# TensorE used as two engines of 64 rows, from the first projection to the end of attention

## The chip, the cores and the metric

The kernel runs on one core of a Trainium2 chip. The metric is the device time of one execution in microseconds (us). Three runs of the kernel before took 1952.63, 1952.87 and 1954.74 us; the median is 1952.87 us.

A core has a matrix engine (TensorE, PE in the profile) that multiplies a stationary operand, loaded by a weight load (PEld), with a moving operand that streams past it; three engines for elementwise work (VectorE or DVE, ScalarE or ACT, GpSimd or POOL); and queues that issue DMA transfers (SP's, here, carries nearly all). Operands lie in SBUF, with the contraction on its 128 partitions; products are accumulated in PSUM and moved out by ACT or DVE.

## The reference

x is 2048 tokens by 576 features. The block computes attention and a gated MLP on the same normalised input.

```python
xn = layernorm(x)
# A: sliding-window attention, 32 heads of 18, window 256, causal
q, k, v = split_heads(xn @ wqkv)                 # wqkv: 576 x 1728
scores = einsum("bhqd,bhkd->bhqk", q, k) * 18**-0.5
p = softmax(where(0 <= i - j < 256, scores, -1e9))
s = merge_heads(p @ v) @ wo
# B: gMLP
z = gelu(xn @ w_in)                              # w_in: 576 x 4608
z1, z2 = z[..., :2304], layernorm(z[..., 2304:])
g = w_sp @ z2 + b_sp                             # over tokens, 2048 x 2048
return x + s * silu((z1 * g) @ w_out)
```

## The kernel before, in words

Every projection is computed from a high and a low part: a value is rounded (`split`, L112: ACT copies with rounding, DVE subtracts) and the product is hi*hi + hi*lo + lo*hi. The normalised input is kept transposed, features on partitions, as nine "planes" in the six tiles b0 to b5 (`plane`, L185): four high planes of 128 features, four low ones, and one that holds the last 64 features, high part above and low part below. A projection of 576 features is then the 14 matmuls that `passes` yields: three for each of four planes, and two for the ninth plane, whose two halves hold different parts.

The stages, in order:

1. Queries and keys (`qk_chunk`, L293): for each of four chunks of 512 tokens the input is normalised and transposed (`norm_chunk`), then nine blocks of 128 columns of q and k are formed by 14 matmuls of 512 tokens each (L312; the first two blocks at L306). Each result is split and stored to DRAM (st_d) in an order that puts a head's 18 features side by side. Weights come in by `load_wqkv`.
2. Values (`v_matmuls`, L504): 16 token tiles, 14 x 2 matmuls of 288 columns each, stored to v_d. They fill gaps of stage 1; what is left follows it.
3. z2 (L720): six pieces of 384 columns by 16 token tiles, 14 matmuls each, then gelu and the statistics of the second layernorm. POOL meanwhile forms sums of blocks of w_sp (`sp_combos`). Near the end the row maxima of the first attention unit are taken.
4. Attention and z1 together (the loop from L796): 16 units, each four heads by half of the tokens. A unit has 32 row-maximum products (`row_max`, L428: queries stationary, keys moving, 128 x 384 or 128 x 256; DVE adds the mask and takes the maximum, L432), a negated maximum that goes out through DRAM and back into two more rows of the query tile, score products (`scores`, L554: keys stationary, queries moving, up to 384 columns; ACT takes the exponential, L558; POOL cuts the band's edges, L562 and L565) and the products with the values (`pv`, L578), in which four heads of 32 output columns each stand side by side in the array. A head's q and k hold 56 rows of 128 (hi and lo parts, the maximum and ones); the other rows of its query tile are zero, so that a 128-row matmul takes one head. z1 = 18 blocks of 128 columns by four chunks of 512 tokens by 14 matmuls (L484) fills the time between.
5. The output projection (L910), the spatial product over tokens (L1150) and the final projection (L1243).

In stages 3 and 4 the order on PE, POOL and DVE is the order in which the program issues the work (`manual_schedule`); in stage 4 ACT and SP too. In stage 4 a small planner writes that order: it keeps a clock, adds an assumed cost for each matmul (`spend`; MM = 227 ns for 512 columns), keeps assumed times at which ACT and DVE will be done, gives every score and maximum product a due time spread over the unit, and fills with z1 matmuls whenever none is due or ready. Score products and row-maximum products have two PSUM banks each (`tps`, `sps`), z1 has two (`mmp`). Products with the values are made for two key blocks at a time (PVN).

## Time and profile before

| | |
|---|---|
| median of three runs | 1952.87 us (1952.63 to 1954.74) |
| span of the profiled execution | 1949.2 us |
| its instructions | 30859, of them 11159 matmuls and as many weight loads |
| PE busy / DVE / ACT / POOL | 1931.0 / 1050.1 / 897.2 / 283.5 us |

The profile gives the profiled execution by its span, from its first to its last instruction; the median of the runs is 3.7 us longer than that, and what lies around the span of this one execution is not shown apart. In the profile "mean ns of one" of a matmul is its latency, from its start to a modelled end; matmuls overlap, so that the time that one costs in a row of them is read from the distance of starts, or from a merged piece of the chain of work. A row like "L720 PE MATMUL mm<-z2wh,b 128*128 128x384 x720" reads: line 720, stationary operand of 128 rows by 128 columns, 384 moving columns, 720 times.

### The profile page before, as it was taken

The numbers are of one execution on the slowest core, as the hardware profiler recorded it, in microseconds if no ns is written. First come the engines' busy times: TensorE is split into PE (matmuls) and PEld (weight loads), VectorE is DVE, ScalarE is ACT, GpSimd is POOL, SyncE is SP. The second block draws the span as 40 slices with busy tenths as digits, with TensorE's granted clock in tenths as the row PEclk, the third lists the DMA queues.
The fourth block names the chain that finished last, engine by engine and source line by source line (L and its number), as shares of the span: only waits on it lengthen the run. The fifth ranks groups of instructions, "written<-read, shape, count | busy, mean of one in ns | idle before, by whom it ended". The sixth has DMA issues, their size and how long they took to land.

```text
span 1949.2 us, 30859 instructions
## 1 busy us (share of the span) xinstructions
PE 1931.0 (99%) x11159; PEld 1656.4 (85%) x11159; DVE 1050.1 (54%) x2294; ACT 897.2 (46%) x1674; POOL 283.5 (15%) x362
## 2 busy tenths in 40 slices
PE   8999999999999999999999999999999999999999
PEld 7889999997777777777698888888888888899998
DVE  5511233366666666665226787757876567663222
ACT  4222322215555556566557675555554534442111
POOL 5001366103222222323200000000000000000000
PEclk9999999999999999999999999999999999999999
DMA  8655799424554556564567777776677555875441
GB/s 266 175 149 157 256 352 349 168 80 137 143 160 135 164 142 160 138 149 127 179 226 253 251 234 249 230 234 214 200 245 240 185 174 186 266 235 160 140 143 58
DMA packets 221513, 375.60 MB, mean 193 GB/s; under 512 B 43312, under 2 KB 118448, under 8 KB 221232
## 3 DMA queue, kind: packets, MB, share of 16 engines
q1 hardware_dynamic: 206000, 349.66, 57.9%
q10 hardware_dynamic: 15360, 23.97, 3.3%
q8 instruction: 88, 1.44, 0.3%
q14 instruction: 65, 0.53, 0.1%
HBM read 260.45 MB, written 112.83 MB: 192 GB/s over the span
## 4 chain that ended last, share of the span: by engine, by line
PE 91%; DMA 3%; DVE 2%; issue 2%; ACT 1%; POOL 1%; SPq 0%; ACTq 0%; DVEq 0%; POOLq 0%
PE acc L1150 32%; PE mm L484 12%; PE po L1243 12%; PE mm L720 9%; PE mm L312 6%; PE sp L428 5%; PE tps L554 5%; PE ops L578 4%; PE vps L504 3%; PE wops L910 3%; DMA a<-in_w_sp_dram 1%; DVE spl L114 1%; DMA zr<-z_d 1%; DMA sc_d<-a 0%; PE tpt L281 0%
## 5 line engine op out<-in xcount | busy, mean ns | idle before, releaser
L1150 PE MATMUL acc<-spl,zh 128*128 128x512 f32 x1008 | 392.6, 389 | 1.1 <-DVE spl L114 0.8
L1150 PE MATMUL acc<-sph,zl 128*128 128x512 f32 x1008 | 392.2, 389 | 0.0
L1150 PE MATMUL acc<-sph,zh 128*128 128x512 f32 x1008 | 392.2, 389 | 0.0
L432 DVE CUSTOM_DVE_ANT_0 junk<-sp,band 128x384 bf16<-128x384 f32 (+1 forms) x512 | 269.6, 538 | 160.4 <-PE sp L428 153.0
L558 ACT ACTIVATE pt<-tps 128x384 f32<-128x384 f32 (+2 forms) x576 | 243.7, 437 | 178.5 <-PE tps L554 168.8
L484 PE MATMUL mm<-b,z1wh 128*128 128x512 f32 x648 | 230.3, 395 | 0.0
L1150 PEld LDWEIGHTS acc<-spl,zh 128*128 128x128 f32 x1008 | 189.2, 188 | 41.7 <-DVE spl L114 2.8
L1150 PEld LDWEIGHTS acc<-sph,zh 128*128 128x128 f32 x1008 | 189.2, 188 | 39.4
L1150 PEld LDWEIGHTS acc<-sph,zl 128*128 128x128 f32 x1008 | 189.2, 188 | 39.1
L114 DVE TENSOR_TENSOR spl<-spr,sph 128x1024 fp32r<-128x1024 f32 x168 | 205.2, 1221 | 30.7 <-ACT sph L113 28.4
L113 ACT ACTIVATE zh<-b 128x384 fp32r<-128x384 f32 x168 | 87.5, 521 | 230.4 <-PE acc L1150 230.3
L720 PE MATMUL mm<-z2wh,b 128*128 128x384 f32 x720 | 191.4, 335 | 1.8 <-ACT zt L730 1.8
L554 PE MATMUL tps<-att 128*128 128x384 f32 (+1 forms) x576 | 184.3, 326 | 0.8 <-ACT pt L558 0.7
L428 PE MATMUL sp<-att 128*128 128x384 f32 (+1 forms) x512 | 177.1, 350 | 1.1 <-DVE mx L432 0.8
L113 ACT ACTIVATE sph<-spr 128x1024 fp32r<-128x1024 f32 x168 | 175.9, 1047 | 1.6 <-DMA spr<-sc_d 1.4
L114 DVE TENSOR_TENSOR zl<-b,zh 128x384 fp32r<-128x384 f32 x168 | 92.9, 553 | 149.7 <-ACT zh L113 144.3
L1243 PE MATMUL po<-b,yh 128*128 128x288 f32 x840 | 147.1, 295 | 0.5 <-ACT gs L1230 0.5
L731 DVE BATCH_NORM_STATS2 st<-zt 128x6 f32<-128x384 f32 x96 | 53.5, 559 | 167.7 <-ACT zt L730 167.7
L484 PE MATMUL mm<-b,z1wl 128*128 128x512 f32 x360 | 142.0, 395 | 0.0
L428 PEld LDWEIGHTS sp<-att 128*128 128x128 f32 x512 | 95.3, 187 | 51.0 <-issue 25.7
L720 PE MATMUL mm<-z2wl,b 128*128 128x384 f32 x400 | 133.7, 334 | 0.0
L720 PEld LDWEIGHTS mm<-z2wh,b 128*128 128x128 f32 x720 | 130.4, 188 | 3.0 <-ACT zt L730 3.0
(187 smaller groups left out, 2872.7 us busy)
## 6 DMA issues: line engine op xcount, KB each, us to landing
spr<-sc_d SPq DMA_DIRECT2D x96, 512.0 KB
spr<-in_w_sp_dram SPq DMA_DIRECT2D x72, 512.0 KB
zr<-z_d SPq DMA_DIRECT2D x144, 192.0 KB
st_d<-qkhl SPq DMA_DIRECT2D x72, 256.0 KB
z_d<-zt ACTq DMA_DIRECT2D x48, 384.0 KB
z_d<-z1o SPq DMA_DIRECT2D x72, 256.0 KB
z1t<-z_d SPq DMA_DIRECT2D x72, 256.0 KB
y_d<-z1t SPq DMA_DIRECT2D x72, 256.0 KB
```

Of the source, the lines that this page charges most:

```text
L113: act.activation(hi, src, AF.Copy)
L114: dve.tensor_tensor(lo, src, f32(hi), ALU.subtract)
L312: pe.matmul(ps, w, r, start=n == 0, stop=n == len(pl) - 1)
L428: pe.matmul(ps[:, :w], q_of(u, j)[:, i * P:(i + 1) * P], k_of(u, j)[:, k0:k0 + w], start=True, stop=True)
L432: dve.tensor_tensor_reduce(out=junk[:, :w], in0=ps[:, :w], in1=band[:, m0:m0 + w], scale=1.0, scalar=-3.0e38, op0=ALU.add, op1=ALU.max, ac ...
L484: pe.matmul(ps, w, r, start=n == 0, stop=n == len(pl) - 1)
L554: pe.matmul(ps[:, :m * P], k_of(u, j)[:, (kb - base) * P:(kb - base + 1) * P], q_of(u, j)[:, (a - lo) * P:(a - lo + m) * P], start=True, s ...
L558: act.activation(pt[:, j, d0:d0 + n * P], ps[:, (qa - a) * P:(qa - a + n) * P], AF.Exp, scale=scale)
L578: pe.matmul(o_ps[c][32 * j:32 * j + 32, (lo - 4 * c) * P:(hi - 4 * c + 1) * P], vgs[u][:, kb - k0, j * VW:j * VW + 32], pt[:, j, (lo - kb) ...
L720: pe.matmul(ps[:, :ZW], r, wt, start=n == 0, stop=n == len(pl) - 1)
L1150: pe.matmul(acc[j], z[:, ps], w[:, cs], start=s == i == 0 and n in OPENS, stop=s == 7 and i == 2, skip_group_check=True)
L1243: pe.matmul(po[i][:, a, :288], y if ahead else y[:, i * P:(i + 1) * P], w[a], start=f == 0 and m == 0, stop=f == NF - 1 and m == 2)
```

## The change

The array is addressed as two row halves: a matmul whose operands lie on partitions 0 to 63 uses the upper 64 rows, one on partitions 64 to 127 the lower 64 rows, each into a PSUM bank of its own.

- The input's planes are now 18, nine high and nine low, of 64 features each. The two halves of the partitions hold different tokens for the same features. Weights are laid out twice, the same 64 rows on both halves (`_twice`, `_blocks`), and are loaded as 9 x 128 columns instead of 5 x 128.
- Projections are made in 27 steps (9 planes by three products), and each step is two matmuls of 64 rows, one for each half, into two banks (`steps_on`, `moving_x`, `moving_w`). Stage 1: q and k blocks 0 to 4 of the first half of the tokens in 10 pairs of 256 tokens (`qk_narrow`), the rest in 13 pairs of 512 (`qk_wide`), with stores of 128 tokens a piece; four blocks of weights are loaded a second time. Values: two column halves by eight token pairs of 288 columns. z2: six pieces by eight token pairs of 384 columns. z1: 18 blocks by two halves of the tokens, by two rows.
- The transposes of the input take 64 rows each, 144 of them instead of 80.
- A head's q and k take 64 partitions, two heads to a tile; the zero rows are gone. Row maxima and scores of a pair of heads can run on the two row halves; the value products are as before.
- The planner keeps a clock for each row half (`row_time`); a value product or the transposition of the maxima takes both. The differences of the z1 weights move from DVE to POOL.
- Stages 1 to 3: PE's order is by hand in stage 1 too; ACT's and SP's in stage 3 (and in the values' part). The stores of v and z2 move from ACT's queue to SP's. The values no longer fill gaps of stage 1.
- Before the output projection three of eight loads of attention output are issued instead of four; the others follow inside it.

```diff
-SLOT = 2 * HS + HS + 256
+SLOT = HS + HS + 256
+    ROWS = (slice(0, 64), slice(64, 128))
+    def moving_x(wh, wl, ps, h):
+        r = ROWS[h]
+        for k in range(9):
+            yield wh[r, k], plane(k, ps)[r]
+            yield wh[r, k], plane(9 + k, ps)[r]
+            yield wl[r, k], plane(k, ps)[r]
+    def steps_on(banks, n, operands):
+        both = [list(ms) for ms in operands]
+        for i in range(STEPS):
+            for h in range(2):
+                pe.matmul(banks[h][:, :n], *both[h][i], start=i == 0, stop=i == STEPS - 1)
+            yield i
...
-        def passes(wh, wl, xs):
-            for k in range(4):
-                yield wh[:, k], plane(k, xs)
-                yield wh[:, k], plane(4 + k, xs)
-                yield wl[:, k], plane(k, xs)
-            yield wh[:, 4], plane(8, xs)
-            yield wl[:, 4], plane(8, xs)
...
+            def qk_wide(j, b):
+                cs = slice(b * 512, (b + 1) * 512)
+                banks = pair_banks()
+                yield from steps_on(banks, 512, [moving_x(*wq[j], cs, h) for h in range(2)])
+                for h in range(2):
+                    hl = pA.tile([P, 2, 512], F32R, name="qkhl", bufs=3)
+                    split(hl[:, 1], hl[:, 0], banks[h])
+                    keep(j, b, h, hl)
...
             def q_of(u, j):
-                t = slots[(2 * u + j // 2) % NSLOT]
-                return t[:, (j % 2) * HS:(j % 2 + 1) * HS]
+                b = 64 * (j % 2)
+                return slots[(2 * u + j // 2) % NSLOT][b:b + 56, 0:HS]
...
+                pe.matmul(ps[:, :w], q_of(u, j)[0:54, i * P:(i + 1) * P], k_of(u, j)[0:54, k0:k0 + w],
+                          start=True, stop=True)
+                spend(j % 2, MM * w / 512 + 4)
...
-                    jobs.append(partial(dve.tensor_tensor, wl[:, ks], raw[:, ks], f32(wh[:, ks]), ALU.subtract))
+                    jobs.append((partial(pool.tensor_tensor, wl[:, ks], raw[:, ks], f32(wh[:, ks]), ALU.subtract),
+                                 "pool", 1000))
...
+                    while any(d for ds in due for d in ds) or (u + 1 == NU and any(q > 0 for q in quota)):
+                        r = 0 if row_time[0] <= row_time[1] else 1
+                        clock = row_time[r]
...
+                        if len(todo) >= PVN and clock >= todo[PVN - 1][0] and (
+                                full or max(bank_free) > clock or len(todo) > PVN):
+                            pv_run(PVN)
                             continue
...
-                if 4 <= n < 8:
-                    oraws.append(wo_load(n))
+                if n in (0, 2, 4, 6, 8):
+                    oraws.append(wo_load(3 + n // 2))
```

719 lines of the change are left out of this document (406 added, 313 removed).

## The prediction

> **What bounds the kernel now.** I read the page's engine rows first, then the busy times by stage, then the chain of waits, then single instructions. The stages are: to 25 us the start; to 200.3 queries, keys and values; to 441.4 z2; to 962.5 attention with z1; then what the change leaves alone.
>
> ```profile
> span 1949.2 us, 30859 instructions
> PE 1931.0 (99%) x11159; PEld 1656.4 (85%) x11159; DVE 1050.1 (54%) x2294; ACT 897.2 (46%) x1674; POOL 283.5 (15%) x362
> PEclk9999999999999999999999999999999999999999
> ```
>
> ```profile
> 0.00:25.00 25.00, 18.93 (x112) 16.34 (x113) 12.67 (x41) 11.86 (x17) 17.06 (x22) 1.00 1.01 309
> 25.00:200.30 175.30, 175.30 (x984) 154.76 (x985) 55.31 (x116) 43.88 (x88) 21.10 (x31) 1.00 0.60 167
> 200.30:441.40 241.10, 239.28 (x1379) 237.80 (x1378) 91.70 (x196) 58.73 (x116) 87.99 (x66) 1.00 0.69 243
> 441.40:962.50 521.10, 519.22 (x3484) 389.48 (x3482) 311.83 (x1101) 312.73 (x738) 157.31 (x244) 1.00 0.53 147
> ```
>
> The columns of the second view are the stretch, then busy time and count of PE, PEld, DVE, ACT and POOL, the granted clock, the share of the DMA engines and GB/s. After the start PE is never idle, at full clock, and no other engine is over 60% in any stage. So up to 962.5 us only fewer or shorter PE slots make this kernel faster. How PE's time divides in attention is shown by the chain of waits there:
>
> ```profile
> by line: PE mm L484 44.2%; PE sp L428 18.7%; PE tps L554 17.8%; PE ops L578 16.6%; DMA den<-ou 1.0%; DVE junk L432 0.4%; PE sp L438 0.4%; issue 0.3%; DVE ou L616 0.2%; ACT pt L558 0.2%; ACT att L113 0.1%; PE mm L720 0.1%; DVE den L600 0.1%;
> ```
>
> Of 521.1 us these are 230.3 for z1, 97.4 for row maxima, 92.8 for scores, 86.5 for value products and 14.1 for the rest. What one matmul costs in a row of them is read from the chain's merged pieces (start, length, count):
>
> ```profile
> 95.91 3.22 PE mm L312 x14
> ...
> 166.59 34.00 PE vps L504 x257
> ...
> 270.62 127.58 PE mm L720 x732
> ```
>
> That is 230 ns for 512 columns, 132.3 for 288 and 174.3 for 384. For 256 the instructions in order of time have two starts 110 to 120 ns apart; I take 115:
>
> ```profile
> 626.39 0.28 PE L428 MATMUL sp<-att 128*128 128x256 f32 x1
> 626.50 0.62 PE L484 MATMUL mm<-b,z1wh 128*128 128x512 f32 x2
> 626.96 0.28 PE L554 MATMUL tps<-att 128*128 128x256 f32 x1
> 627.17 1.50 PE L578 MATMUL ops<-pt,vg 128*32 128x384 f32 x16
> ```
>
> **Do halves of the array run side by side?** No 64-row matmul is in this trace, but value products use the array in four parts of 32 columns. The last row above has 16 of them, 384 columns each, in 1.50 us: 94 ns each, where a whole-array matmul of 384 columns takes 174. The weight loads:
>
> ```profile
> 627.17 0.16 PEld L578 LDWEIGHTS ops<-pt,vg 128*32 128x32 f32 x8 [0.25 <-issue]
> 627.52 0.13 PEld L578 LDWEIGHTS ops<-pt,vg 128*32 128x32 f32 x4 [0.19 <-issue]
> ```
>
> ```profile
> L578 PEld LDWEIGHTS ops<-pt,vg 128*32 128x32 f32 x1402 | 36.6, 109 | 37.1 <-issue 31.1 <-POOL pt L565 0.7
> L484 PEld LDWEIGHTS mm<-b,z1wh 128*128 128x128 f32 x648 | 118.3, 188 | 8.9
> ```
>
> Four loads of 109 ns each are through in 0.13 us, so they overlap. Parts of the array do work at once, loads included. I carry this over from column parts to row halves; that is the step on which the forecast stands, and the rivals price its failure. I take a pair of 64-row matmuls at the time of one 128-row matmul of the same columns.
>
> **Queries, keys, values (to 200.3 us).** Before: 9 x 4 x 14 = 504 matmuls of 230 ns, 115.9 us. After: 13 x 27 = 351 pairs of 512 columns, 80.7, and 10 x 27 = 270 of 256, 31.1: together 111.8, so -4.1. Values: 16 x 14 x 2 = 448 at 132.3 ns, 59.3, become 2 x 8 x 27 = 432 pairs, 57.2: -2.1. Transposes:
>
> ```profile
> 10.09 0.93 PE L281 MATMUL tpt<-ident,xr 128*128 128x128 f32 x7
> ```
>
> Less the last one's latency of 0.27 us, six starts lie 0.11 us apart; 80 cost 8.8 us. The 144 of half the rows and columns cost 4.0 (72 pairs at half of 0.11) to 15.8 (one by one, no shorter); I take no change, nearest to 72 pairs at 0.11. The values no longer fill holes here, so a late weight or a full store buffer shows on PE. DMA:
>
> ```profile
> st_d<-qkhl SPq DMA_DIRECT2D x72, 256.0 KB
> ...
> xr<-in_x_dram SPq DMA_DIRECT2D x16, 288.0 KB
> ...
> wraw<-in_wqkv_dram SPq DMA_DIRECT2D x9, 480.0 KB
> ```
>
> The row for 25 to 200.3 us has 167 GB/s at a share of 0.60, so some 278 GB/s at full share. The ten narrow blocks last 31 us and in that time move ten stores of two such 256 KB, six weight blocks of 9 x 128 x 128 x 4 bytes (590 KB) and four rows of input, 10 MB: 36 us by that rate. I put 5 us for this on the path (none, if the start's 309 GB/s holds; 10, if the smaller pieces of the stores slow them). The wide blocks need 234 GB/s on average, under the limit. Stage: -4.1 - 2.1 + 5, about **-1** (from -11 to +16).
>
> **z2 (to 441.4).** 6 x 16 x 14 = 1344 matmuls of 174.3 ns become 6 x 8 x 27 = 1296 pairs: -8.4. The first unit's 32 row maxima become 16 slots, -2.8. ACT's gelu, DVE's statistics and the stores are as many as before, with ACT at 59 of 241 us and DMA at 0.69; the weights' further 18 x 270 KB are 5 MB in 230 us, 21 GB/s beside 243, hidden. Stores of z2 now queue behind weight loads on SP, and a waiting store holds what stands behind it there; the next piece's weights have a whole piece (38 us) to arrive, so I cost this at nothing. **-11**.
>
> **Attention with z1 (to 962.5).** z1: 1008 matmuls become 18 x 2 x 27 = 972 pairs, 230.3 x 972/1008 = 222.1: -8.2. Row maxima and scores: 190.2 us, two heads in one slot: -95.1. Two things take some of it back. First, not all of the 190.2 is matmul:
>
> ```profile
> L428 PE MATMUL sp<-att 128*128 128x384 f32 x424 | 150.8, 361 | 1.1 <-DVE mx L432 0.8
> L554 PE MATMUL tps<-att 128*128 128x384 f32 x384 | 128.9, 343 | 0.0
> L554 PE MATMUL tps<-att 128*128 128x256 f32 x192 | 55.3, 291 | 0.8 <-ACT pt L558 0.7
> L428 PE MATMUL sp<-att 128*128 128x256 f32 x56 | 16.1, 287 | 0.0
> ```
>
> 808 x 174.3 + 248 x 115 ns is 169.4; 20.8 us are waits in front of them (a bank not yet free). PE takes its matmuls in one order, so such a wait stops both rows and is not halved: +10.4. Second, a value product needs both rows. Its two-block calls are about 72; before each, one row waits on average half a z1 matmul, 115 ns, which is half of that for the whole: +4. Value products stay: 86.5, drains included. The planner's 4 ns for a product beyond its columns, 20 before, moves due times, not work. The other engines: ACT gains 18 x (1152 - 640) columns of weight rounding, about 8 us on 312.7. DVE loses the z1 weight differences to POOL, where 960 columns take 2.2 us:
>
> ```profile
> L493 DVE TENSOR_TENSOR z1wl<-z1raw,z1wh 128x256 fp32r<-128x256 f32 x34 | 16.4, 484 | 9.3 <-ACT z1wh L493 9.3
> L493 DVE TENSOR_TENSOR z1wl<-z1raw,z1wh 128x128 fp32r<-128x128 f32 x17 | 6.2, 364 | 0.0
> L332 POOL TENSOR_TENSOR wlq<-wraw,whq 128x960 fp32r<-128x960 f32 x4 | 8.9, 2242 | 1.4 <-ACT whq L247 1.4
> ```
>
> DVE falls from 312 to 289, POOL rises from 157 by 54 x 0.9 to 206. In the new stage of 432 us that is ACT 74%, DVE 67%, POOL 48%: late next is ACT's exponential, but on average there is room. Sum: -8.2 - 95.1 + 14.4 = **-89** (to -103 if nothing is lost at the pairing).
>
> After 962.5 us nothing changes but the time of five loads, each two token tiles ahead of its use. **Sum:** -1 - 11 - 89 = -101 from a span of 1949.2 is 1848; the median stands 3.7 above this profile, so 1852.
>
> **A rule that speaks against it.** The two load rows differ by 79 ns for 96 columns, 0.82 ns a column, so 128 columns take about 105 ns beside a fixed part; and the 64-row loads still have 128 columns. The Trainium skill ("TensorE: Matmul & The Clock Gate", section "LDWEIGHTS (loading the stationary operand)") says that a load's time goes by its columns, at 1.2 a nanosecond, and that rows do not matter. By it, were the halves to load by turns, a pair would need 213 ns and the time would come to about 1993. The trace agrees with the column rate; whether halves take turns it does not show.
>
> **Rivals.**
> - *Loads of the two halves take turns* (slower). A pair then costs at least two loads, 210 ns. Free under 512-column pairs (230), it adds to z2 1296 x 36 ns = 46, values 432 x 78 = 34, narrow blocks 270 x 95 = 26, and 416 score and maximum slots of 384 (36 ns) and 128 of 256 (95 ns), 27: +133, **1985**. It decides from 198 ns a pair, where the price reaches the 101 us gained. Against it: the overlapping loads of value products.
> - *ACT's idle time cannot shrink.* It waits for scores in the shape the order gives:
>
> ```profile
> L558 ACT ACTIVATE pt<-tps 128x384 f32<-128x384 f32 x384 | 182.8, 491 | 109.7 <-PE tps L554 101.3 <-POOL pt L562 2.4 <-POOL pt L565 1.8
> ```
>
>   With the shorter forms it stands idle 169 us for scores. If two banks for two rows keep that, the stage is 321 + 169 = 490, -31 in place of -89: **1910**. For it: two rows fill both banks at once. Against: at 490 PE would idle, and the planner puts z1 there.
> - *Row halves do not overlap.* Every pair counts twice: z1 972 x 230, z2 1296 x 174, values 57, queries 112, slots 87 add 705 us: some **2557**. The change would not do what it says. Against it: the 94 ns of the column parts.
>
> **How the numbers follow.** The forecast, 1830 to 1880 by the bounds of its terms, 0.58; ACT's idle time, in part or whole, 1880 to 1915, 0.23; loads by turns 0.11; no overlap 0.05; a start or stage 1 held up by DMA beyond its bound together with waits in attention, 0.03. About 0.2% (4 us) is what a measurement can tell from no change; hardly a case lies there, 0.01. Faster 0.83, slower 0.16. Range 1825 to 1915, which leaves out 0.19.
>
> **What would show it.** Right: z2 still at 174 ns per pair, its stage near 230 us; attention near 432 with the chain shares of L428 and L554 halved. Loads by turns: pairs of 288 columns at 210 ns. ACT: PE idle in front of score loads, released by the exponential. Wrong above all if a 64-row pair is not one slot, or if stage 1 waits for stores.

## The result, and the profile after

The changed kernel takes 2030.61 us (median; 2020.26 to 2035.15), the kernel before 1953.8 us beside it on the same chip: a ratio of 1.0377, with a 95% interval from 1.0346 to 1.0409. The forecast was 1852 us and faster; the range ended at 1915. The kernel became 3.8% slower.

The page of the changed kernel, its first row and the rows of PE and of the granted clock:

```profile
span 2033.4 us, 37956 instructions
PE 1926.1 (95%) x14552; PEld 1649.8 (81%) x14552; DVE 1055.0 (52%) x2301; ACT 908.1 (45%) x1746; POOL 346.7 (17%) x421
PEclk7988999999999999999969999999999999999999
```

Two things are new. PE, which was busy for 99% of the span, is idle for 107 us; and the row of the clock, all nines before, has sevens, eights and a six. Busy times by stage, in the same columns as before (stretch, PE, PEld, DVE, ACT, POOL, granted clock, DMA share, GB/s):

```profile
0.00:25.00 25.00, 13.48 (x108) 12.02 (x110) 18.22 (x52) 9.19 (x16) 13.45 (x18) 0.75 0.70 248
25.00:247.40 222.40, 192.45 (x2195) 179.82 (x2197) 62.20 (x138) 59.95 (x132) 40.25 (x40) 0.91 0.59 156
247.40:489.70 242.30, 236.18 (x2633) 231.28 (x2629) 103.77 (x218) 62.97 (x147) 89.86 (x69) 0.99 0.80 262
489.70:1043.30 553.60, 503.37 (x4423) 366.75 (x4423) 292.29 (x1054) 306.00 (x739) 203.19 (x295) 0.93 0.55 149
1043.30:2033.40 990.10, 980.58 (x5208) 859.94 (x5200) 578.56 (x841) 470.00 (x715) 0.00 (x0) 0.99 0.63 206
```

Queries, keys and values now end at about 248 instead of 200.3 us (+47), z2 takes 242 instead of 241 (+1), attention with z1 556 instead of 523 (+33, counted in both from the first z1 matmul to the first matmul of the output projection; the view of before above is 2 us shorter), and what follows is 3.5 us longer. In attention no engine but PE is over 56% busy, and PE itself has 50 us of idle time at a clock of 0.93.

From the trace I took two sums for each stage: the distances of more than 0.6 us between the starts of consecutive matmuls ("gaps"; the distance from a stage's last matmul to the next stage is left out), and the time for which the clock's record stands at one half. Where PE works, half of that time is lost; where the half clock lies inside a gap, the gap has counted it already. A stage less its gaps, less half of its half-clock time outside the gaps, is what its matmuls and their small waits need at full clock ("rest"):

| stage of the changed kernel | length | gaps | half clock | of it in gaps | rest | length before | rest before |
|---|---|---|---|---|---|---|---|
| queries and keys | 175.9 | 35 | 44 | 16 | 126 | 200.4 (with values) | 196 (with values) |
| values | 71.7 | 10 | 10 | 2 | 58 | | |
| z2 | 242.1 | 7 | 7 | 2 | 232 | 241.2 | 239 |
| attention with z1 | 555.9 | 71 | 84 | 16 | 450 | 523.3 | 521 |

In the kernel before the gaps of the three stages were 4.9, 2.5 and 2.3 us, and the clock was never halved in them. All in all the changed kernel spends 154 us at half clock, 36 of them inside gaps, so that the clock costs 59 us (2 before). The 84 us by which its span is longer are then 115 us more of gaps and 57 more from the clock, less 89 us that matmuls and small waits need less.

**The halves do run side by side.** Instructions of z2 in order of time (start, length):

```profile
259.71 0.33 PE L206 MATMUL ma<-att,b 64*128 64x384 f32 x1
259.84 0.33 PE L206 MATMUL mb<-att,b 64*128 64x384 f32 x1
259.88 0.33 PE L206 MATMUL ma<-att,b 64*128 64x384 f32 x1
260.02 0.33 PE L206 MATMUL mb<-att,b 64*128 64x384 f32 x1
260.05 0.33 PE L206 MATMUL ma<-att,b 64*128 64x384 f32 x1
```

The upper half (ma) starts every 0.17 us and the lower (mb) within the same time: a pair costs what one matmul of 128 rows did (174 ns). The weight loads of the two halves lie over each other, 0.18 us each and started 0.04 us apart:

```profile
259.67 0.18 PEld L206 LDWEIGHTS mb<-att,b 64*128 64x128 f32 x1
259.71 0.18 PEld L206 LDWEIGHTS ma<-att,b 64*128 64x128 f32 x1
259.85 0.18 PEld L206 LDWEIGHTS mb<-att,b 64*128 64x128 f32 x1
```

**What the clock does behind a gap.** Four stretches around the start of attention's second unit, same columns: before the gap, the gap, and twice 6.5 us behind it:

```profile
526.00:532.34 6.34, 6.30 (x54) 4.04 (x53) 4.13 (x18) 3.39 (x10) 2.37 (x4) 1.00 0.26 85
532.34:535.89 3.55, 0.40 (x5) 0.03 (x1) 0.61 (x3) 0.00 (x0) 1.79 (x2) 0.81 0.07 16
535.89:542.50 6.61, 6.61 (x45) 5.06 (x47) 1.93 (x7) 2.66 (x6) 1.23 (x2) 0.59 0.64 161
542.50:549.00 6.50, 6.50 (x61) 4.33 (x57) 4.10 (x19) 4.07 (x11) 1.23 (x2) 1.00 0.69 190
```

A gap of 3.55 us is followed by 6.6 us at 0.59 of the clock, in which PE is busy all the time and does 45 matmuls, where the next stretch of that length has 61. The gap costs its own length and nearly 3 us more.

**What opens the gap.** The instructions in order of time at that place: the transposition of the unit's maxima, their put to DRAM, the fetch back into the query tiles, the unit's first scores:

```profile
531.32 0.28 PE L517 MATMUL sp<-ident,mx 128*32 128x128 f32 x1
...
532.42 0.49 SPq L525 DMA_DIRECT2D m_d<-mhl  x1
534.23 1.14 SPq L530 DMA_DIRECT2D att<-m_d  x4
...
535.89 0.66 PE L623 MATMUL tps<-att 56*128 56x384 f32 x1 [3.15 <-DMA att<-m_d]
```

That way takes 4.6 us, and the unit's scores stand at its end. In the kernel before the transposition and the first scores of a unit lay 6.2 to 8.4 us apart (17.4 at the first unit; 7.8 in the rows below), and no matmul of that trace waits for the fetch:

```profile
623.94 0.27 PE L438 MATMUL sp<-ident,mx 128*32 128x128 f32 x1
...
631.72 0.34 PE L554 MATMUL tps<-att 128*128 128x384 f32 x1
```

Now a unit has the same 32 maxima, the same way and less PE work to cover it. The waits (us in all, times, longest):

```profile
PE tps L623 <- DMA att<-m_d: 27.7, 11, 5.1
PE sp L504 <- DMA att<-st_d: 12.2, 7, 3.9
...
SPq L530 <- DMA m_d<-mhl: 50.2, 16, 7.6
```

The third row is SyncE, which carries nearly all transfers in one order: it stands in front of each fetch until the put has landed, and all loads and stores behind it stand too. From the transposition to the first scores the units of the changed kernel take 4.4 to 11.3 us.

**What opens the gaps of the first stage.** ACT and DVE work in the way of the bank evictions; the waits of PE before 247 us, and what ACT stood in front of at lines of the values' weights:

```profile
PE ma L206 <- DVE qkhl L116: 16.9, 5, 4.6
PE ma L206 <- ACT ve L804: 9.3, 3, 5.4
PE tpt L308 <- DVE xpair L298: 6.6, 2, 6.2
...
ACT wvh L269 <- DMA wraw<-in_w_v_dram: 30.2, 3, 10.8
ACT wv1h L269 <- DMA wraw<-in_w_v_dram: 21.3, 3, 10.4
```

The rounding of a block of weights stands on ACT right behind the issue of its load; for up to 10.8 us ACT waits for the transfer, and the evictions that PE needs stand behind it. In the kernel before values and queries were mixed and one filled the holes of the other.

### The profile page after: what moved, and what is told of

The parts are those of the page before. It is cut to its first block, busy times and chain, and to the rows that moved or that the text cites. A ratio compares the mean times of both kernels' runs of the same rounds, so it can differ in the third digit from the quotient of the medians.

```text
span 2033.4 us, 37956 instructions
## 1 busy us (share of the span) xinstructions
PE 1926.1 (95%) x14552; PEld 1649.8 (81%) x14552; DVE 1055.0 (52%) x2301; ACT 908.1 (45%) x1746; POOL 346.7 (17%) x421
## 4 chain that ended last, share of the span: by engine, by line
PE 76%; DMA 13%; DVE 4%; ACT 3%; SPq 3%; issue 2%; POOL 0%; ACTq 0%; DVEq 0%; POOLq 0%
PE acc L1289 32%; PE po L1382 11%; PE mb L206 7%; PE ma L570 6%; PE mb L570 5%; PE ma L206 5%; PE ops L651 4%; PE tps L623 3%; PE sp L504 2%; DMA att<-st_d 2%; DMA m_d<-mhl 2%; PE wops L1049 2%; DMA wraw<-in_w_v_dram 1%; DMA z1wh<-in_w_z_dram 1%; DMA xr<-in_x_dram 1%
## 5 line engine op out<-in xcount | busy, mean ns | idle before, releaser
L627 ACT ACTIVATE pt<-tps 128x384 f32<-128x384 f32 (+2 forms) x576 | 233.4, 440 | 193.6 <-PE tps L623 164.1
L570 PE MATMUL mb<-b,z1wh 64*128 64x512 f32 x648 | 231.0, 413 | 0.1
L570 PE MATMUL ma<-b,z1wh 64*128 64x512 f32 x648 | 229.3, 413 | 0.2 <-ACT zt L841 0.2
L623 PE MATMUL tps<-att 56*128 56x384 f32 (+1 forms) x576 | 176.9, 375 | 38.7 <-DMA att<-m_d 27.7
L504 PE MATMUL sp<-att 54*128 54x384 f32 (+1 forms) x512 | 167.1, 368 | 14.1 <-DMA att<-st_d 12.2
L623 PEld LDWEIGHTS tps<-att 56*128 56x128 f32 x576 | 97.4, 195 | 89.6 <-issue 45.3
L635 POOL TENSOR_SCALAR_AFFINE_SELECT pt<-pt 128x512 f32<-128x512 f32 x128 | 82.4, 644 | 298.8 <-ACT pt L627 298.7
L570 PE MATMUL ma<-b,z1wl 64*128 64x512 f32 x324 | 133.2, 411 | 0.0
L570 PE MATMUL mb<-b,z1wl 64*128 64x512 f32 x324 | 132.9, 410 | 0.0
L570 PEld LDWEIGHTS ma<-b,z1wh 64*128 64x128 f32 x648 | 123.9, 196 | 4.9 <-ACT zt L841 0.4
```

The costliest lines, as they stand in the source:

```text
L504: pe.matmul(ps[:, :w], q_of(u, j)[0:54, i * P:(i + 1) * P], k_of(u, j)[0:54, k0:k0 + w], start=True, stop=True)
L570: pe.matmul(ps, w, x_, start=n == 0, stop=n == STEPS - 1)
L623: pe.matmul(ps[:, :m * P], k_of(u, j)[:, (kb - base) * P:(kb - base + 1) * P], q_of(u, j)[:, (a - lo) * P:(a - lo + m) * P], start=True, s ...
L627: act.activation(pt[:, j, d0:d0 + n * P], ps[:, (qa - a) * P:(qa - a + n) * P], AF.Exp, scale=scale)
L635: pool.affine_select(out=pt[:, :, 0:P], in_=pt[:, :, 0:P], pattern=[[0, 4], [1, P]], compare_op=ALU.is_ge, fill=0.0, base=0, channel_multi ...
```

## The experiments

### One suspect at a time: maxima, values' weights, buffers, start

Maxima a third earlier in the unit, and transposed as soon as the last is taken (RM1 places the last of them in the unit before):

```diff
-RM1 = 0.765
+RM1 = 0.60
...
+                        if any(taken.get(v) == 2 * RMN and clock >= all_max[v] + 100 for v in maxima):
+                            pv_run(0)
+                            continue
```

> The row maxima's due times end at 0.60 of a unit instead of 0.765, and their transposition is issued as soon as the last maximum of the unit is taken. Theory A (the maxima's way through DRAM, some 5 us from the transposition to the score products, is longer than what is left of the shorter units): the 33 us in which score products wait for that transfer go, and with them most of the half-clock time behind them, so attention falls from 553 us to about 505 and the total by 40 to 50. Theory B (the units are paced by scores, exponentials and value products, and the wait only shows where the slack of that chain ends): attention falls by under 15 us.

Values' weights rounded two blocks behind the issue of their load:

```diff
...
-                    load_wv(wv, n - 4, pA, pool)
+                    formers.append(load_wv(wv, n - 4, pA, pool))
+                if n in (6, 7, 8):
+                    formers.pop(0)()
```

> The values' weights are rounded on ACT two blocks after their load is issued instead of right behind it. Theory A (ACT waits for the load with the evictions of PE's banks queued behind it): the six PE gaps of 3 to 6 us between 127 and 203 us go (21 us), and about 10 us of half clock with them; total 20 to 30 us less. Theory B (stage 1 is held by its stores, at 0.88 of the DMA engines): the gaps move to other waits, under 8 us less.

Four instead of three buffers for exponentials (one z1 output buffer less; the planner's limits follow):

```diff
-                    pts[u, kb] = ap_.tile([P, 4, 384], F32, name="pt", bufs=3)
+                    pts[u, kb] = ap_.tile([P, 4, 384], F32, name="pt", bufs=4)
...
```

> Four buffers for the exponentials of a key block instead of three (and three for z1's results instead of four, to make room). Theory B (the chain scores, exponentials, edge cuts, value products with three buffers paces a unit): attention falls by 25 to 35 us, above all in the second eight units with their ten key blocks. Theory A: shorter plans only wait longer for the maxima, under 10 us less.

The low parts of the first two weight blocks on DVE instead of POOL:

```diff
-                return partial(pool.tensor_tensor, wl, raw, f32(wh), ALU.subtract)
+                return partial((dve if j < 2 and 1 not in xpair else pool).tensor_tensor, wl, raw, f32(wh), ALU.subtract)
```

> The low parts of the first two weight blocks are formed on DVE after the first norm, not on POOL beside it. If POOL's long subtractions hold up DVE's small operations at the start (two of them took 2.0 and 2.5 us where they took 0.15 before), the first transposes start at about 12 us instead of 15.9 and the total falls by 4 to 8 us. If the input's loads are what is late, nothing changes.

| | time, us | ratio to before | attention | gaps | half clock |
|---|---|---|---|---|---|
| e1, maxima early | 2022.95 | 1.0346 [1.0331, 1.0361] | 537.3 | 63 | 58 |
| e2, weights later | 2016.36 | 1.0294 [1.0255, 1.0334] | 549.8 | 68 | 81 |
| e3, four buffers | 2024.43 | 1.0351 [1.0336, 1.0366] | 541.7 | 64 | 81 |
| e4, lows on DVE | 2028.1 | 1.0366 [1.0340, 1.0391] | 549.1 | 67 | 77 |

The intervals of e1, e3 and e4 overlap that of the changed kernel (1.0346 to 1.0409), so that by their total times none of the three can be told from it; e2 can. The lengths of stages are from one profiled execution each. In attention, which neither e2 nor e4 nor, further below, e6 touches, these show 550, 549 and 545 us and the changed kernel 556: a difference of some 11 us there says nothing.

e2 is the cleanest: the values' stage falls from 71.7 to 58.0 us, with 0.8 us of gaps and without half clock (57.2 was its forecast by pairs). That is theory A for half of the gaps it named; the three near 128, 140 and 152 us stay, and the total falls by 14 instead of 20 to 30 us. e1 brings attention down by 19 us; scores wait 16.2 instead of 27.7 us for maxima, and the gaps shrink by 8 us and the clock's cost by 10. Neither of its two theories had that: the maxima's way is a part, not the whole. e3 has 14 us less in attention, between its theories and little more than profiles differ by, although the waits for maxima grow to 35.4 us; that units held by the buffers now meet the maxima earlier would explain it, and is not tested apart. e4 missed. The first transposes come at 15.2 instead of 15.92 us, since DVE itself now spends 1.35 and 1.34 us on the subtractions in the middle of the normalisation.

### The clock and ACT's order

Six unread matmuls in front of each pair of scores of the last unit, which has too few z1 matmuls left:

```diff
...
+                        if u == NU - 1 and not r:
+                            keep_warm(6)
                         scores(u, *steps[n[0]], n[1])
```

> One edit to the changed kernel: in the last attention unit six matmuls of 384 columns, 1.04 us, whose result nothing reads, stand before each pair of score products; 20 pairs, 21 us of added PE work. Theory C (PE's clock falls to half when the unit leaves it idle, and that costs as much as the idle time itself): the 31 us at half clock in that unit go, and the unit, some 43 us long, is no longer than before in spite of the added work, or up to 8 us shorter. Theory D (the clock only follows, the unit is paced by ACT): the unit stays or grows by up to 21 us.

The time is 2039.22 us (1.0431 [1.0415, 1.0447]). The last 31 us of the changed kernel's last unit, and then the last unit of e5, in the columns of the stages:

```profile
1019.00:1050.00 31.00, 26.71 (x124) 16.34 (x124) 6.76 (x9) 11.19 (x24) 5.35 (x8) 0.50 0.49 136
```

```profile
1003.00:1053.00 50.00, 46.59 (x307) 31.52 (x308) 6.87 (x10) 22.51 (x47) 9.29 (x15) 0.99 0.34 95
```

The clock stays up, as meant. But from the last transposition of maxima to the output projection it takes 66.6 instead of 53.8 us: of the 21 us that were added some 8 came back. That is theory D. The 8 us can be the clock's, or idle time that the added matmuls fill; the run does not part them. That the unit is paced by the chain from scores over exponentials and cuts to the value products fits this, and is not tested apart.

The last nine blocks of queries and keys with ACT, DVE and SP in an order by hand (with e2's edit): loads are issued ahead of a block, and their rounding stands behind the block's evictions:

```diff
...
+            early_order.close()
+            early_order.enter_context(tc.manual_schedule(engines=ENGINES | {ET.Activation, ET.SP}))
             for n, j in enumerate((4, 5, 6, 7, 8, 0, 1, 2, 3)):
+                if n < 4:
+                    formers.append(load_wq(n))
+                if n in (4, 5, 6):
+                    formers.append(load_wv(wv, n - 4, pA, pool))
                 for _ in qk_wide(j, 1):
                     pass
+                if n < 7:
+                    formers.pop(0)()
```

> As e2, and in the last nine blocks of queries and keys ACT, DVE and SP keep the order of the program too, with each weight block's load issued before a block and rounded after that block's evictions. Theory A (ACT waits for a load with evictions behind it): the three gaps of 3 to 4 us near 128, 140 and 152 us that e2 left go, with the half clock behind them: 15 us less than e2. Theory B (stores saturate DMA there): the gaps only move; within 5 us of e2.

1998.16 us (1.0220 [1.0193, 1.0247]). Between 100 and 160 us there is no gap over 1 us and no half clock left; queries and keys fall from 175.9 to 159.9 us. The waits of PE there in the changed kernel, and in e6:

```profile
PE ma L206 <- DVE qkhl L116: 9.7, 3, 3.7
```

```profile
PE mb L206 <- DVE qkhl L116: 0.2, 1, 0.2
```

So those gaps were an order of work and loads, as theory A has it (18 us below e2). Which of the three engines' orders did it the run does not part. The loads kept up: DMA's share in that stretch was not the limit.

Two combinations followed: e1, e2 and e3 together (with a smaller allowance for z1 ahead of its share, SLACK 4 instead of 24), and the same with e6's order.

> e1, e2 and e3 in one kernel, and at most 4 z1 steps a row ahead of a unit's share instead of 24, so that the last unit keeps more of them. If the three causes are separate, their gains add: 2030 - 14 - 14 - 10 and some 10 us of half clock in the last unit, 1975 to 1990. If one hides another: above 2000.

> e7 with the hand order of e6: 15 us below e7 if the gaps of stage 1 are ACT's order, equal to e7 if they are DMA's. Below 1955 it would beat the kernel before; by the sums I expect 1960 to 1975.

They take 1992.86 (1.0198 [1.0175, 1.0221]) and 1982.88 us (1.0142 [1.0126, 1.0157]); attention is 528.1 and 528.2 us, with 49 and 48 us of gaps. e7 is 3 us above the range in which the gains add. The hand order takes another 10 us off, of the 15 that were expected, and e8 misses its 1960 to 1975.

### The maxima's way, the start, another queue

```diff
-                    rows = m_d[u].rearrange("(n j i) q -> n j (i q)", n=2, j=4)
+                    rows = m_d[max(u - 1, 0)].rearrange("(n j i) q -> n j (i q)", n=2, j=4)
```

> The changed kernel, but the scores of a unit are shifted by the maxima of the unit before (read from DRAM with the same transfers, which landed some 25 us earlier); the softmax is the same for any shift, only the guard against overflow is changed. All matmuls, maxima, transposes and transfers stay, and the wait of a unit's first scores for its own maxima is gone. Theory A (the way of the maxima through DRAM, and the half clock behind each of these waits, are what the attention lost): waits of scores on it were 27.7 + 5.5 us on TensorE, the queue behind SyncE's wait some 10 us more, and with the half clock behind some ten of them (3.4 to 6.8 us at half clock each, so 17 to 34 us) attention falls from 556 to about 495 us and the time to about 1970. Theory B (ScalarE's chain of exponentials and cuts paces the units, the maxima wait only fills slack): attention stays above 540, the time above 2010.

2002.6 us (1.0243 [1.0214, 1.0273]), attention 527.7 with 57 us of gaps and 50 of half clock: between the theories, and for a reason that the waits show:

```profile
PE tps L623 <- DMA att<-m_d: 15.8, 8, 5.3
...
SPq L530 <- DMA m_d<-mhl: 3.4, 1, 3.4
```

SyncE no longer stands in front of the fetch (3.4 instead of 50.2 us). The fetch is still behind the put in SyncE's order, though, and the put waits for the unit's own maxima; so half of the wait is left. What the edit removes, one landing per unit, is worth 28 us: 14 us less of gaps and 16 less from the clock.

The start by hand: a version of e8 in which POOL's subtractions begin only when the first chunk is normalised, and statistics stand in pieces between the evictions (the core of it):

```diff
+            for _ in norm_chunk(0):
+                pass
+            pool.tensor_copy(warm, xpair[0][1][:, 8, 1, 63:64])
+            forms[0]()
+            forms[1]()
...
             for j in range(5):
                 for _ in qk_narrow(j, 1):
                     pass
+                some(norm, (2, 1, 2, 3, 0)[j])
```

> The version with all mends so far (earlier maxima, four exponential buffers, values' weights rounded later, hand order in the last nine blocks: 1982.9 us), with ScalarE, VectorE and SyncE also put in an order by hand from the first instruction on: POOL's subtractions start after the first chunk is normalized, the statistics of a chunk are placed between the bank evictions in pieces, the first two blocks end one after the other, more warm-up transposes. Theory A (the gaps of 7.2, 4.5, 2.5 and 3.1 us and the half clock up to 60 us are an order of ScalarE and VectorE, not loads of the halves): gaps above 1.2 us in the first 62 us fall from 21 us to under 6, half clock from 24 us to under 7, stage of q and k from 160 to about 137, time about 1960. Theory B (loads of x and weights limit the start whatever the order): q and k stay above 152 us, time above 1974.

1955.59 us (1.0009 [0.9994, 1.0024]), no longer to be told from the kernel before: theory A. Queries and keys take 140.4 us; against e8 gaps are 7 instead of 24 us and half clock 10 instead of 31. Two DVE instructions of the changed kernel's normalisation, and the POOL instruction that ran beside them:

```profile
9.51 5.19 POOL L364 TENSOR_TENSOR wql<-wraw,wqh 128x1152 fp32r<-128x1152 f32 x2 [5.84 <-ACT wqh L261]
```

```profile
10.14 2.01 DVE L124 TENSOR_SCALAR tm<-tm 128x2 f32<-128x2 f32 x1
12.19 2.53 DVE L125 TENSOR_TENSOR rs<-rs,tm 128x2 f32<-128x2 f32 x1
```

The same two in e10, with POOL held back:

```profile
11.84 0.17 DVE L124 TENSOR_SCALAR tm<-tm 128x2 f32<-128x2 f32 x1
12.05 0.16 DVE L125 TENSOR_TENSOR rs<-rs,tm 128x2 f32<-128x2 f32 x1
```

Two instructions on two numbers a partition took 2 us and more until POOL's subtraction let go: they end at 12.15 and 14.72 us, and POOL's two at about 12.1 and 14.7. e4 shows it by that one edit: with POOL free the same two took 0.15 to 0.16 us. So e4's premise held, though its gain did not come. This agrees with the Trainium skill ("SBUF — State Buffer", section "SBUF: two separate sides"), by which GpSimd and some VectorE instructions, those with two inputs in SBUF among them, share a pair of ports as an exclusive lock for a whole instruction; the loser waits.

e10 with the maxima's put and fetch on ACT's DMA queue (and z1's weights requested 7 steps earlier):

```diff
-                    sp.dma_start(m_d[u], f32(m))
+                    act.dma_start(m_d[u], f32(m))
...
-                        sp.dma_start(f32(q_of(u, j)[54:56, :]), rows[:, j])
+                        act.dma_start(f32(q_of(u, j)[54:56, :]), rows[:, j])
```

> e10, and the maxima are put to DRAM and fetched back by ScalarE's DMA queue instead of SyncE's, and the load of the next z1 weights is issued 7 steps earlier. Theory A (the maxima are late because the small transfers stand behind large ones in SyncE's queue): put to landing falls from 5 to 8 us at the worst units to about 2, the waits on maxima fall under 8 us, attention from 528 to about 505. Theory B (the landing is slow in whatever queue, or ScalarE waiting for the landing holds up its exponentials): attention 520 to 545.

1986.74 us (1.0168 [1.0142, 1.0193]), attention 557.5: the way of theory B, and 12 us beyond its range. ACT waits for landings now, and its exponentials stand behind that:

```profile
ACT pt L668 <- DMA att<-m_d: 31.1, 7, 5.8
```

### Gaps that move

e10 with unread matmuls in the gaps at the starts of units (the table gives their number by unit):

```diff
+KEEP = {0: 24, 1: 12, 3: 20, 4: 6, 6: 14, 9: 5, 10: 9, 11: 21, 12: 12}
...
+                        if n == (0, 0) and u in KEEP:
+                            keep_warm(KEEP[u])
```

> e10 (1955.6 us) with 5 to 24 unread matmuls of 384 columns (0.175 us each, 123 in all, 21.5 us, sized to 0.8 of the measured gap) just in front of the first scores of the nine units that began with a gap of over 1.2 us (together 25.3 us). Work and waits stay as they are, only TensorE is not idle in these gaps. Theory A (a gap costs twice: its own length and 3.4 to 6.8 us at half clock behind it): attention's half-clock time falls from 45 us to about 20, attention from 527 to about 514, time about 1943, though matmuls were added. Theory B (the clock only falls where the unit has nothing to do anyway): no gain, or a loss of up to 10 us where the added matmuls make the scores late: 1955 to 1965.

e10 with scores forbidden in the plan until 6.4 us behind the transposition of the unit's maxima, so that z1 matmuls stand there (and z1's weights requested earlier); then the same with value products after every key block:

```diff
...
-                    return (done_max if kind else done_exp)[-2] + 60
+                    if kind:
+                        return done_max[-2] + 60
+                    return max(done_exp[-2] + 60, md_at.get(u, 0) if u else 0)
```

> e10, with the planner told that a unit's scores may not begin before 6.4 us after its last maximum is transposed (the measured 5.5 us from put to first scores, and the transposition), so that it puts z1 matmuls there instead of a wait, and the z1 weights' load issued 7 steps earlier. Theory A (the attention's loss is work in the wrong place: units too short for the maxima's way, gaps, half clock): waits on maxima fall from 32 us (e11's count, 18 to 25 in e10) to under 8, gaps above 0.6 us from 49 to about 30, half clock from 45 to under 25, attention from 527 to about 500, time about 1930. Theory B (z1 work put at the units' start is then missing in their middle, and the gaps move there): attention 520 to 530, time 1950 to 1960.

```diff
-PVN = 2
+PVN = 1
```

> e13, and value products are issued after one key block instead of two, so that the three or four exponential buffers come free sooner, at the price of more meetings of the two rows (some 72 more calls at 0.11 to 0.22 us, 8 to 16 us). Theory A (buffers of exponentials pace the units of the second half): attention 8 to 15 us under e13. Theory B (meetings of the rows cost more than the buffers give): attention 0 to 15 us above e13.

| | time, us | ratio to before | attention | gaps | half clock | rest |
|---|---|---|---|---|---|---|
| e10 | 1955.59 | 1.0009 [0.9994, 1.0024] | 526.8 | 49 | 45 | 459 |
| e12 | 1968.9 | 1.0069 [1.0054, 1.0084] | 540.6 | 40 | 29 | 489 |
| e13 | 1956.84 | 1.0000 [0.9985, 1.0016] | 533.9 | 44 | 49 | 469 |
| e14 | 1958.04 | 1.0013 [1.0004, 1.0022] | 529.7 | 45 | 39 | 467 |

e12 falsifies its theory A. The gaps shrink by 10 us and the clock's cost by 7, yet attention is 14 us longer: the added 21.5 us stand in the sum, and another 9 with them. Half clock is a price of a gap, but keeping PE busy with nothing doesn't buy it back when the units are held by something else. e13 points at what that is. The waits for maxima fall from 22.3 (in e10) to 9.3 us, and the next one grows from 8.5 to 25.6, that of the maxima's matmuls for the next unit's queries and keys. Attention ends 4 us above the range of its theory B:

```profile
PE sp L545 <- DMA att<-st_d: 25.6, 12, 6.3
PE tps L665 <- DMA att<-m_d: 9.3, 5, 4.6
```

e14's single value products show 4 us less in attention, which one profile each cannot tell from nothing, and nothing in the time; neither theory's range holds.

### The chain of a unit, spread over two units

A unit's second pair of heads is loaded in the first 8 us of the unit before it, then come its sixteen maxima at some 0.83 us, the transposition, and 5 to 6 us through DRAM: some 27 us that do not get shorter when PE gets faster. If that holds the units, a sixth buffer for the q and k of a pair of heads must help, for then everything can be loaded and half of the maxima taken one unit earlier. It is paid for with an exponential buffer and with the output projection's spare tile, which moves into the sixth buffer. From e14, without e13's rule for the start of scores:

```diff
-NSLOT = 5
...
-EARLY = 4
-RM2 = 0.81
-RM1 = 0.60
+NSLOT = 6
...
+EARLY = 8
+RM2 = 0.55
+RM1 = 0.55
...
-                    pts[u, kb] = ap_.tile([P, 4, 384], F32, name="pt", bufs=4)
+                    pts[u, kb] = ap_.tile([P, 4, 384], F32, name="pt", bufs=3)
...
-                    jobs = [(lambda it=it: next(it, None)) for p in (2 * u + 3, 2 * u + 4) if p < 2 * NU
+                    jobs = [(lambda it=it: next(it, None)) for p in ([3] if u == 0 else []) + [2 * u + 4, 2 * u + 5] if p < 2 * NU
```

> e14, but with six instead of five buffers for the q and k of a pair of heads (paid for by three instead of four exponential buffers, and by a buffer of the output projection that now lies in the sixth), both pairs of a unit are loaded a whole unit earlier, sixteen instead of eight maxima of a unit are taken in the unit before the last, and the last of them at 0.55 of the unit; no rule of a minimum time any more. Theory A (a unit cannot be shorter than its chain: loads of the second pair some 8 to 10 us after the unit's start, sixteen maxima at 0.83 us, the transposition and 5.5 to 6.4 us through DRAM, together 28 to 30 us, whatever TensorE does; with the chain spread over two units it lets go): waits on maxima and on loads (10.5 + 15.6 us in e14) fall under 6 us together, half clock of attention from 39 to under 20 us, attention from 530 to about 495, time about 1925. Theory B (exponentials and their buffers pace the units, and there is one buffer less now): attention 525 to 545, time 1955 to 1975.

The second run has PVN = 2, EARLY = 6 and both RM at 0.60:

> As e15, with value products issued after two key blocks and twelve early maxima, the last at 0.60. With three exponential buffers Theory A of e15 expects attention some 5 to 15 us above e15 (the buffers come free later, but the rows meet less often) and still under 515; Theory B 540 to 560.

e15 takes 1939.38 us (0.9923 [0.9907, 0.9938]) and is 0.8% faster than the kernel before. Attention is 507.2 us with 27 us of gaps and 31 of half clock; the wait for loads is down to 2.9 us, that for maxima still at 16:

```profile
PE tps L664 <- DMA att<-m_d: 16.0, 9, 4.3
PE sp L545 <- DMA att<-st_d: 2.9, 2, 2.6
...
SPq L571 <- DMA m_d<-mhl: 82.5, 14, 7.2
SPq L723 <- DMA r_d<-den: 44.7, 15, 5.1
```

Theory A holds in direction, with 12 us missing to its 495. e16 takes 1956.15 us (0.9998 [0.9983, 1.0014]), attention 535.5: neither theory's range. With three exponential buffers the value products after two key blocks cost far more than the meetings of the rows they save; since e16 also takes fewer maxima early, the 28 us between the two are not all from that.

The two SyncE rows above are the last suspect: 127 us in which the queue stands in front of a fetch until its put has landed, with all transfers behind it. In e17 the fetches are issued when the put will have landed; e18 also takes the maxima a little earlier.

```diff
-                for ns in (wait, wait + 2600):
+                for ns in (wait, wait + 5600):
...
-                    after(put_inverse() + 4800, get_inverse)
+                    after(put_inverse() + 7500, get_inverse)
```

> e15 (1939.4 us, attention 507.2), with the fetch of the maxima issued 5.6 instead of 2.6 us after their put, and the fetch of the denominators' inverses 7.5 instead of 4.8 us after theirs, so that SyncE no longer waits in front of them for a landing and the loads and stores behind it go on. Theory A (what is left of the wait on maxima, 16 us in 9 waits, is SyncE's queue standing still behind such fetches): the waits of scores on maxima fall under 8 us, SyncE's waits in front of both fetches from some 60 and 40 us to under 30 together, attention to about 495, time about 1928. Theory B (the later issue only makes the maxima later by as much): waits on maxima 15 to 30 us, attention 505 to 520, time 1938 to 1950.

```diff
-RM2 = 0.55
-RM1 = 0.55
+RM2 = 0.5
+RM1 = 0.5
```

> e17 with the last maxima of a unit at 0.50 instead of 0.55 of the unit before, and the early ones from there on: 1 to 2 us more reserve in front of the scores of most units. Theory A of e17: within 5 us of e17. Theory B: 5 to 15 us under e17, since the reserve is what lacks.

e17 takes 1919.83 us (1917.63 to 1923.63): 0.9827 of the kernel before, interval 0.9812 to 0.9842. Its page, busy times of attention, and waits:

```profile
span 1918.6 us, 37993 instructions
PE 1879.3 (98%) x14574; PEld 1596.3 (83%) x14574; DVE 1051.8 (55%) x2301; ACT 905.6 (47%) x1746; POOL 348.0 (18%) x423
```

```profile
440.00:931.00 491.00, 475.67 (x4424) 332.01 (x4423) 294.51 (x1054) 305.35 (x742) 204.63 (x296) 0.99 0.61 167
```

```profile
PE tps L664 <- DMA att<-m_d: 8.7, 4, 4.6
...
SPq L571 <- DMA m_d<-mhl: 19.9, 9, 7.5
SPq L723 <- DMA r_d<-den: 19.3, 10, 4.5
```

SyncE stands 39 instead of 127 us, scores wait 8.7 instead of 16 us for maxima, and attention falls to 491.1 us with 18 us of gaps and 14 of half clock: theory A. A later fetch left shorter waits for its data, while what stood behind it went on. e18 takes 1928.77 us (0.9873 [0.9852, 0.9894]), attention 501.0, which is slower than e17 and in neither theory's range: the reserve was not what lacked.

## Why the prediction was wrong

- **The step on which it stood held.** "A pair of 64-row matmuls at the time of one 128-row matmul": 174 ns a pair in z2, 57.3 us for the 432 pairs of the values where nothing holds them (e7; 57.2 forecast). The rivals of loads by turns and of no overlap are out. The part of the Trainium skill's rule that was weighed there ("TensorE: Matmul & The Clock Gate", section "LDWEIGHTS (loading the stationary operand)"), a load's time by its columns whatever the rows, may hold for one load (a 64-row load of 128 columns shows 184 ns); but the two halves load at the same time, so it sets no price on a pair.
- **The matmuls alone came out near the forecast, not at it.** At full clock and without gaps z2 is 232 us (230 forecast). Attention is 450, where 432 and the 2 us to the output projection were forecast: 71 us of the 89 are there. That the rest is the same in e1, e2, e4 and e6 (450 to 451), whose gaps run from 63 to 71 us and half clock from 58 to 84, bears out the way of counting. Of the length of attention e17 takes off 32 us.
- **The step that failed** is the term for the waits in front of maxima and scores, "such a wait stops both rows and is not halved: +10.4", with the sentence further down, "late next is ACT's exponential, but on average there is room". It took the waits of a trace in which PE was always late and carried them over to a PE that is no longer late. What came in their place is 71 us of gaps and 34 us from the clock (half of the 68 at half clock outside the gaps). "On average there is room" is true of every engine (none over 56%), and decides nothing: a unit is held by a chain of latencies (loads, maxima, transposition, the way through DRAM) that the change left as it was, while the work that covered it was cut. Three edits at that chain, with all the matmuls left in, took 28 (e9), 22 (e15 against e14) and 16 us (e17 against e15) off attention. The 6.2 to 8.4 us between the transposition of a unit's maxima and its scores stood in the trace of before; the text never asked what would become of them.
- **The clock was not in the sum at all.** The row of nines was read off, and the text did not ask whether it would stay once PE has idle time. Up to the end of attention 124 us of gaps went with 55 us lost to the clock outside them, over 0.4 for each.
- **Stage 1** was forecast at -1 (bound +16; the terms given add up to +11) and came out at +47. The sentence "the values no longer fill holes here, so a late weight or a full store buffer shows on PE" named the danger, and then priced it by DMA's bytes (5 us). The bytes were no trouble; the order on ACT, DVE, POOL and SP was: 45 us of gaps (5 before) and 18 from the clock. With that order mended (e10) queries, keys and values take 202 us, near the 199 forecast.
- **z2** came out at +1, not -11: 6 us less of matmuls and small waits, but gaps of 7 us (2.5 before) and 2.6 from the clock. The longest gap is one of 3.36 us at the first row maxima, which wait for queries and keys.
- **The rival "ACT's idle time cannot shrink"** had the kind right (latency between engines, not their load), but put attention at 490 us and the time at 1910, where the changed kernel shows 556 and 2031. It named only one link: with one more buffer for exponentials attention was 14 us shorter (e3, little more than profiles differ by), with work at the maxima's way and SyncE's queue more (e9 and e17, above). That e17's attention is 491 us is no support for its figure, since e17 is another kernel. What of the remaining 57 us between e17's attention and the forecast is the meeting of the two rows and what small waits is not settled: gaps and clock explain 24 of them.

Not tried: whether the same mends help the kernel before (its gaps up to the end of attention are 9.7 us in all), and maxima that do not go through DRAM.

## What to carry to other kernels

A change that makes the busiest engine faster also removes the cover under which all other latencies lay. Before summing up the savings, list each transfer or hand-over that returns just in time (here: maxima through DRAM, a way of 4.4 us or more with 6.2 to 8.4 us to cover it), and ask for each what covers it afterwards; the busy shares of the other engines do not answer that. In this kernel a gap had to be priced with the half-clock time behind it; and a queue that works in order and waits for its own transfer delays everything behind it, so that issuing a fetch later can make the waits shorter (e17).

## What the runs showed of the hardware that was not expected

- The clock's record changes only on a grid of 3.41 us. In the changed kernel the 22 stretches at half clock inside its work last 3.4 or 6.8 us but for two (17.1 and 30.7 us, five and nine steps), each directly behind gaps. Every step of that grid at full clock in which PE was busy for less than half was followed by half clock, none in which it was busy for over 0.72 was, and between 0.53 and 0.72 both occur. So not the length of a gap alone decides, but also how it lies on the grid: one of 2.0 us (at 756.5 us) was enough, and so were three of 0.8 to 1.3 us in a row (at 965 us), while one of 2.8 us (at 563.7 us) and one of 2.5 us (at 656.1 us), each spread over two steps, were not. Other runs have exceptions, such as a fall in e10 behind a step busy for 0.89.
- The Trainium skill ("TensorE: Matmul & The Clock Gate", section "Part 1: The HAM clock gate") has the array at half rate after an idle window of about 3.4 us until a busy one. The step agrees; the trigger is lower here, since steps in which PE was busy for nearly half were enough.
- A put of 32 KB is landed within 1.8 us at 532.42 us of the changed kernel; elsewhere in it SyncE waits up to 7.6 us for one.
- DVE instructions of 0.16 us took 2.0 and 2.5 us beside a POOL subtraction (2.6 us each).
